# An attention, MoE and soft-MoE kernel on one core: v in fp16 parts everywhere, scores from fp16 parts of q and k, and a second expert layer on four column groups

## The chip, the core and the metric

The kernel runs on one core of one Trainium2 chip. The metric is the device time of one execution in microseconds (us); the time before is 681.06 us, the median of three runs (677.28 to 685.23). A core has TensorE (PE, matmuls, its weight loads shown as PEld), VectorE (DVE), ScalarE (ACT), GpSimd (POOL) and SyncE (SP, which only issues DMAs here). The clock of PE that the chip grants stands beside the busy times as a share of 2.4 GHz; the two levels are 1.2 and 2.4 GHz.

## What is computed

Three stages, one after the other, on 4 batches of 576 tokens (2304 in all) with 8 heads of 64:

```python
scores = scale * np.matmul(q, k.transpose(0, 1, 3, 2))
thresh = np.max(scores, axis=-1, keepdims=True) - tau
scores = np.where(scores >= thresh, scores, -1000000000.0)
attn = np.exp(scores - scores.max(-1));  attn /= attn.sum(-1) + 1e-9
x = np.matmul(attn, v)                       # -> [2304, 512]
h = x @ w_in                                 # [512, 2048]
x = np.maximum(0.01 * h, h) @ w_out          # [2048, 512]
logits = x @ phi                             # 8 experts x 4 slots
slot_input = softmax(logits, over tokens).T @ x
slot_out[e] = np.maximum(slot_input[e] @ w1[e], 0) @ w2[e]    # w1, w2: 8 x 512 x 1024
out = softmax(logits, over slots) @ slot_out
```

All inputs are fp32 (`w_in` and `w_out` arrive as 64 bit numbers and are made into fp32 on the chip). fp32 accuracy is kept either by fp32 matmuls or by splitting an operand into an fp16 part (hi) and the fp16 rest (lo) and multiplying hi by hi, hi by lo and lo by hi.

## The kernel before

The tokens are cut into 18 tiles of 128. Batches are 4.5 tiles long, so tiles 4 and 13 hold rows of two batches. For each tile `attention` computes 8 heads in 4 pairs, `feed` computes the hidden layer (48 matmuls of 512 columns, L1331, in 4 quarters of 12) and the logits, and `block` updates the running sums over two tiles. After the last tile a tail computes the expert layers for the 32 slots and the output.

Each operation is added with a priority, a cost and the engines that may run it; a planner (`Plan.schedule`) then fixes the order of the instructions on every engine, by the costs given and the table `O` of constants. On the chip each engine goes through its own list in that order and waits where an operand or a buffer isn't ready. The buffers are named by tags with a fixed number of slots.

What the change touches:

- **Scores.** `load_qk` loads q and k of one batch and one pair (640 KB, tag `qk`, 8 slots). `heads` multiplies them in fp32, two heads at a time on the upper and lower 64 rows of PE (L1100), into a PSUM tile S of 2 x 512. `ends` does the same for the last 64 keys (L1071). VectorE takes the maximum (L1109), ScalarE applies the threshold (L1125).
- **Weights times v.** `own(t)` says which pairs go by `by_pe`: all four for tiles 0 to 3 (`P0`, `TP=4`), pair 3 alone for the others (`P1`). `by_pe` transposes the weights on PE in fp32 (9 of 128 x 128, L1159), applies exp while ScalarE copies them back (L1164), and multiplies with v in fp32 (5 matmuls a head, L1176). The other pairs go by `by_dma`: exp in place (L1192), a cast to fp16 hi (L1202 on VectorE or L1203 on ScalarE), three subtractions on GpSimd for lo (L1213, 512, 128 and 512 elements long as the trace counts them), a DMA transpose of each head issued by SP (L1226, 9 blocks of 128), and 14 fp16 matmuls of 65 columns a head (L1250). The tag `ah` for hi and lo has 2 slots, `aT` for what is transposed has 3.
- **v.** `split_v` makes the fp16 parts (`vx`) and fp32 copies (`vr`, `vs`) as the pairs need them.
- **Tail.** `load` fetches 64 blocks of 512 KB of w1 and w2 into slots of the tags in `BIG` (27 of them: wh, qk, r, e2, ae, ah), as they become free; the first layer (L1685) multiplies k by k for four experts on four groups of 32 columns of PE; the second layer (L1753) has 32 operations of 4 matmuls, each operation for one expert, that is one group of columns. Blocks of w_out (`wot`) lie in slots of the tags in `SM`, until L1641 has used them.

Of the kernel before, what the change touches and what calls it, by code (L numbers as in the profile page):

```python
# [359 lines left out]
def emit(tc, a, out, dbg=None, opt=None):  # L360
# [73 lines left out]
    for n, p_, k in (  # L434
# [4 lines left out]
        ("qk", "main", O["QK"]), ("vr", "main", O["VR"]), ("vx", "main", O["VX"]), ("vs", "main", O["VS"]),  # L439
# [36 lines left out]
    def dump(name, b, sel, prio=1e9):  # L476
        if dbg and name in dbg:
# [36 lines left out]
    gate8, rt = const([P, 1]), const([P, 1])  # L514
    dve_op(
        P0, 80,
        lambda: dve.tensor_scalar(
            out=gate8.ap, in0=gate.ap, scalar1=0.125, scalar2=None, op0=ALU.mult
        ),
        r=[gate], w=[gate8],  # L520
    )
    dve_op(
        P0, 80,
        lambda: dve.tensor_scalar(
            out=rt.ap, in0=taup.ap, scalar1=8.0, scalar2=None, op0=ALU.mult
        ),
        r=[taup], w=[rt],
    )
# [6 lines left out]
    )  # L535

# [289 lines left out]
    for c in range(FF // P):  # L826
# [21 lines left out]
        pe_op(PQ, 440, f, r=[w, ident], w=[tp])  # L848
# [15 lines left out]
        pe_op(PQ, 850, f, r=[wt, phi], w=[wpp])  # L864
# [102 lines left out]
    qk = {}  # L967

    def load_qk(b, prio, step):
        for pr in range(4):  # L970
            raw = qk[b, pr] = pl.buf("qk", [P, 2, KX])
            dma(
                prio + pr * step, t_dma(P * 2 * KX * 4),
                (lambda pr, raw: lambda dq: dq.dma_start(out=raw.ap, in_=a["qk"][b, pr]))(pr, raw), w=[raw],
            )

    vtiles, vfs, vrs_of = {}, {}, {}

    own = lambda t: O["P0"] if t < O["TP"] else O["P1"]
# [25 lines left out]
    def split_v(b, pr, prio, vr):  # L1005
        sv = svs[b]
        vf = lambda: vr.ap[:, :, 0:D]
# [10 lines left out]
        if any(pr not in own(t) for t in tiles_of(b)):  # L1018
            vx = vtiles[b, pr] = pl.buf("vx", [P, 2, 10, D + 2], F16)
            va = lambda w: vx.ap[:, w, :, 0:D]  # L1020
            q = prio + (O["VD"] if any(pr in own(t) for t in tiles_of(b)) else 0.0)
# [13 lines left out]
            fm = lambda eng: lambda: eng.memset(vx.ap[64:, 1, 8:, 0:D], 0.0)  # L1035
            add_alt(q, [("pool", 180, fm(pool)), ("dve", 110, fm(dve))], w=[(vx, 1)])
            for w in range(2):
                pool_op(
                    q, 100, (lambda w: lambda: pool.memset(vx.ap[:, w, :, D : D + 1], 1.0 - w))(w),
                    w=[(vx, 2 + w)],  # L1040
                )
        if any(pr in own(t) for t in tiles_of(b)):
            vs = vfs[b, pr] = pl.buf("vs", [P, 2, D + 2])
            fc = lambda eng: lambda: eng.tensor_copy(out=vs.ap, in_=vr.ap[:, 8:])
            add_alt(prio, [("pool", 300, fc(pool)), ("dve", 150, fc(dve))], r=[vr], w=[vs])
            fm = lambda eng: lambda: eng.memset(vr.ap[:, 0:8, D : D + 1], 1.0)
            add_alt(prio, [("pool", 100, fm(pool)), ("dve", 110, fm(dve))], w=[(vr, 1)])
            fm = lambda eng: lambda: eng.memset(vs.ap[:, :, D : D + 1], 1.0)
            add_alt(prio, [("pool", 100, fm(pool)), ("dve", 110, fm(dve))], w=[vs])
            for i in range(2):  # L1050
                fm = lambda eng, i=i: lambda: eng.memset(
                    vs.ap[64 - 64 * i : 128 - 64 * i, i, 0 : D + 1], 0.0)
                add_alt(prio, [("pool", 100, fm(pool)), ("dve", 110, fm(dve))], w=[vs])
            vrs_of[b, pr] = vr
# [8 lines left out]

    def ends(t, prio):
        Tp = pl.buf(("misc",), [P, H, KT], F32, "Tp")
        Ts, tn = pl.buf("T", [P, H, KT]), pl.buf("tn", [P, H])

        def f():
            for r0, r1, b, o in regs_of(t):
                for pr in range(4):  # L1070
                    pe.matmul(  # L1071
                        out=Tp.ap[r0:r1, 2 * pr : 2 * pr + 2], lhsT=qk[b, pr].ap[:, 0, o : o + r1 - r0],
                        rhs=qk[b, pr].ap[:, 1, KW:KX], start=(pr == 0), stop=True, skip_group_check=True,
                    )

        pe_op(prio, 900 * len(tile_parts(t)), f, r=[qk[b, pr] for b in tile_parts(t) for pr in range(4)], w=[Tp, Ts, tn])
        act_op(prio, t_act(512), lambda: act.activation(out=Ts.ap, in_=Tp.ap, func=AF.Copy), r=[Tp], w=[Ts])
        dve_op(
            prio, 607,
            lambda: dve.tensor_reduce(out=tn.ap, in_=Tp.ap, axis=AX.X, op=ALU.max, negate=True),  # L1080
            r=[Tp], w=[tn],
        )
        dve_op(
            prio, 75,
            lambda: dve.tensor_scalar(
                out=tn.ap, in0=tn.ap, scalar1=rt.ap[:, 0:1], scalar2=None, op0=ALU.add
            ),
            r=[rt], w=[tn],
        )
        return Ts, tn  # L1090

    def heads(t, pr, prio, ae, flat, Ts, tn):
# [3 lines left out]
        def f():  # L1096
            for r0, r1, b, o in regs_of(t):
                for i in range(2):
                    h = slice(64 * i, 64 * i + 64)
                    pe.matmul(  # L1100
                        out=ps.ap[r0:r1, i], lhsT=qk[b, pr].ap[h, 0, o : o + r1 - r0],
                        rhs=qk[b, pr].ap[h, 1, 0:KW], start=True, stop=True, skip_group_check=True,
                    )

        pe_op(prio, 900 * len(tile_parts(t)), f, r=[qk[b, pr] for b in tile_parts(t)], w=[ps])
# [6 lines left out]
        for i in range(2):  # L1112
# [3 lines left out]
                    out=th.ap[:, i : i + 1], in0=nm.ap[:, i : i + 1], scalar1=rt.ap[:, 0:1],  # L1116
# [13 lines left out]
        tail = lambda: two(ae.ap[:, 2 * KW :]) if flat else ae.ap[:, :, KW:S]  # L1130
        pl.add(
# [15 lines left out]
    def by_pe(t, pr, p, parts, regs, Ts, tn, xa, xbuf):  # L1147
# [5 lines left out]
        def turn(c0, c1, key):  # L1153
# [3 lines left out]
            def f():  # L1157
# [11 lines left out]
        for i, (c0, c1) in enumerate(((0, 4), (4, 8), (8, 9))):  # L1169
            turn(c0, c1, i)  # L1170
# [698 lines left out]
```

## Time and profile before

| | us |
|---|---|
| median of 3 runs | 681.06 |
| the profiled execution | 686.13 |
| its span, first to last instruction | 684.3 |
| PE busy | 612.7 (90% of the span) |
| DVE busy | 406.3 (59%) |
| ACT busy | 399.6 (58%) |
| POOL busy | 172.8 (25%) |
| granted PE clock, mean | 0.939 |

A busy time is that in which at least one instruction of the engine runs. Instructions of one engine overlap, on PE by much: a matmul of 512 fp16 columns is shown with 385 ns, while the next one starts 217 ns after it. So what a group of matmuls takes from PE is read from the time at which the next group starts. SPq stands for SP's list of DMAs.

### The profile page before, as it was taken

Reading aid. Unit: us, or ns where it says so; the run is one execution under the profiler, and the core shown is the slowest. Engines: PE = TensorE matmul, PEld = TensorE weight load, DVE = VectorE, ACT = ScalarE, POOL = GpSimd, SP = SyncE. Lnnn points to the kernel's source line nnn. Section 1 sums busy time; section 2 is a strip of 40 time slices with the busy share of each in tenths; the row PEclk is TensorE's granted clock in tenths of the full one; section 3 lists DMA queues with packets and bytes.
Section 4 is the critical chain, followed back from the end, with each engine's and each line's share of the span. In section 5 each row is a group of like instructions: output and inputs, shape, how many; then the busy total and the mean of one; then the engine's idle time right before and its main releaser. Section 6 shows DMA issues by size and latency. Waiting matters only on the chain.

```text
span 684.3 us, 13565 instructions
## 1 busy us (share of the span) xinstructions
PE 612.7 (90%) x5212; PEld 369.2 (54%) x5212; DVE 406.3 (59%) x992; ACT 399.6 (58%) x745; POOL 172.8 (25%) x253
## 2 busy tenths in 40 slices
PE   4898887999879999999999898999999988489995
PEld 1666555776445656565555554655556643224552
DVE  3978869656757586599886555565767343310011
ACT  4887667776747677688786637576666522211022
POOL 0200100200323256245355323263363200200000
PEclk8798988999989999999999889999999999689997
DMA  8965410455998687899697659677669966839995
GB/s 321 375 221 181 129 61 17 139 159 164 163 214 152 115 143 127 186 190 200 121 177 119 114 89 201 132 133 131 105 123 213 203 131 177 267 109 413 409 408 215
DMA packets 203297, 123.94 MB, mean 181 GB/s; under 512 B 179168, under 2 KB 179680, under 8 KB 203232
## 3 DMA queue, kind: packets, MB, share of 16 engines
q1 hardware_dynamic: 199488, 114.02, 69.1%
q10 hardware_dynamic: 3744, 9.05, 5.5%
q8 instruction: 41, 0.67, 0.4%
q14 instruction: 24, 0.20, 0.1%
HBM read 70.48 MB, written 8.91 MB: 116 GB/s over the span
## 4 chain that ended last, share of the span: by engine, by line
PE 69%; ACT 11%; DVE 7%; DMA 6%; issue 3%; SPq 1%; POOL 1%; ACTq 0%; POOLq 0%; DVEq 0%
PE h L1331 23%; PE S L1100 9%; PE X L1176 6%; PE X L1753 6%; PE X L1250 5%; PE eT L1159 3%; PE misc L1176 3%; DMA aT<-ah 2%; ACT e L1164 2%; PE S L1685 2%; DMA rT<-r 2%; PE misc L1071 2%; PE misc L1525 2%; PE misc L862 2%; ACT g L1343 2%
## 5 line engine op out<-in xcount | busy, mean ns | idle before, releaser
L1331 PE MATMUL h<-wh,xT 128*128 128x512 f16 x864 | 215.0, 385 | 7.5 <-ACT g L1343 6.6
L1213 POOL TENSOR_TENSOR ah<-ae,ah 128x512 f16<-128x512 f32 (+1 forms) x126 | 120.6, 984 | 162.3 <-DVE ah L1202 130.7
L1331 PEld LDWEIGHTS <-xT 128*128 128x128 f16 x864 | 80.4, 100 | 101.7 <-issue 35.2
L1125 ACT ACTIVATE ae<-S,th 128x512 f32<-128x512 f32 x144 | 94.3, 686 | 17.5 <-POOL ah L1213 7.0
L1109 DVE TENSOR_REDUCE nm<-S 128x2 f32<-128x1024 f32 x72 | 87.7, 1219 | 28.2 <-PE S L1100 28.1
L1100 PE MATMUL S<-qk 64*128 64x512 f32 (+1 forms) x320 | 89.1, 690 | 9.6 <-DMA qk<-in_qk 5.9
L1343 ACT ACTIVATE g<-h,c 128x512 f32<-128x512 f32 x72 | 49.5, 687 | 70.0 <-PE h L1331 65.0
L1164 ACT ACTIVATE e<-eT,c,c 128x512 f32<-128x512 f32 (+1 forms) x90 | 60.1, 668 | 27.9 <-PE eT L1159 27.8
L1350 DVE CAST r<-g 128x512 f16<-128x512 f32 x57 | 27.8, 487 | 67.4 <-ACT g L1343 62.8
L1250 PEld LDWEIGHTS <-aT 128*128 128x128 f16 (+1 forms) x1344 | 49.7, 103 | 25.0 <-issue 14.6
L1250 PE MATMUL X<-vx,aT 128*128 128x65 f16 (+1 forms) x1344 | 54.4, 196 | 4.5 <-DMA aT<-ah 4.5
L1159 PE MATMUL eT<-c,ae 128*128 128x128 f32 x270 | 49.7, 296 | 8.7 <-ACT e L1164 8.1
L1192 ACT ACTIVATE ae<-ae,c,c 128x1152 f32<-128x1152 f32 x42 | 56.6, 1348 | 0.8
L1159 PEld LDWEIGHTS eT<-c,ae 128*128 128x128 f32 x270 | 34.1, 151 | 28.8 <-ACT e L1164 18.0
L1176 PE MATMUL X<-vr,e 128*128 128x65 f32 (+1 forms) x352 | 47.1, 281 | 0.0
L1357 DVE TENSOR_TENSOR r<-g,r 128x512 f16<-128x512 f32 x56 | 44.3, 791 | 3.9 <-ACT r L1352 3.0
L1134 POOL TENSOR_TENSOR ae<-T,th 128x128 f32<-128x128 f32 x33 | 15.4, 468 | 122.6 <-DVE th L1115 61.4
L1176 PEld LDWEIGHTS X<-vr,e 128*128 128x128 f32 (+1 forms) x352 | 45.0, 200 | 2.3 <-issue 1.2
L1202 DVE CAST ah<-ae 128x1152 f16<-128x1152 f32 x33 | 25.7, 779 | 20.2 <-ACT ae L1192 14.3
L1100 PEld LDWEIGHTS S<-qk 64*128 64x128 f32 (+1 forms) x320 | 23.2, 190 | 26.7 <-ACT ae L1125 7.8
L1115 DVE TENSOR_SCALAR th<-nm,c,tn 128x1 f32<-128x1 f32 x144 | 31.8, 264 | 0.8
L1376 PE MATMUL misc<-c,rT 128*128 128x64 f16 x288 | 19.1, 191 | 9.6 <-DMA rT<-r 9.2
(288 smaller groups left out, 911.0 us busy)
## 6 DMA issues: line engine op xcount, KB each, us to landing
wh<-in_w SPq DMA_DIRECT2D x21, 512.0 KB, 10.1
qk<-in_qk SPq DMA_DIRECT2D x15, 640.0 KB, 5.5
qk<-in_w SPq DMA_DIRECT2D x18, 512.0 KB, 8.0
r<-in_w_in SPq DMA_DIRECT2D x16, 512.0 KB, 4.1
r<-in_w SPq DMA_DIRECT2D x13, 512.0 KB, 10.2
rT<-in_w_out SPq DMA_DIRECT2D x25, 256.0 KB, 3.4
scr<-w SPq DMA_DIRECT2D x16, 256.0 KB, 3.3
vr<-in_v SPq DMA_DIRECT2D x9, 330.0 KB, 4.4
```

The costliest lines, as they stand in the source:

```text
L1100: pe.matmul(out=ps.ap[r0:r1, i], lhsT=qk[b, pr].ap[h, 0, o : o + r1 - r0], rhs=qk[b, pr].ap[h, 1, 0:KW], start=True, stop=True, skip_group ...
L1109: lambda: dve.tensor_reduce(out=nm.ap, in_=ps.ap, axis=AX.X, op=ALU.max, negate=True),
L1125: (lambda i: lambda: act.activation(out=main()[:, i], in_=ps.ap[:, i], func=AF.Prelu, bias=th.ap[:, i : i + 1], scale=1.0, alpha=2.0**90))(i),
L1159: pe.transpose(tp.ap[:, c - c0], ae.ap[:, c * P : (c + 1) * P], ident.ap)
L1164: lambda: act.activation(out=eT.ap[:, c0:c1], in_=tp.ap, func=AF.Exp, bias=nt.ap[:, 0:1], scale=gate8.ap[:, 0:1]),
L1176: pe.matmul(out=xa(2 * pr + i)[r0:r1], lhsT=eT.ap[:, c, r0:r1], rhs=(vfs[b, pr].ap[:, i] if c == 8 else vrs_of[b, pr].ap[:, c])[:, 0 : D + 1],
L1192: lambda: act.activation(out=ae.ap, in_=ae.ap, func=AF.Exp, bias=nt.ap[:, 0:1], scale=gate8.ap[:, 0:1]),
L1213: lambda: pool.tensor_tensor(out=ah.ap[:, h, w0 : w0 + c1 - c0], in0=ae.ap[:, h, c0:c1], in1=ah.ap[:, h, c0:c1], op=ALU.subtract),
L1250: pe.matmul(out=xa(2 * pr + i)[r0:r1], lhsT=w()[:, r0:r1], rhs=vtiles[b, pr].ap[:, wv, cv, 0 : D + 1], start=(n == 0 and 2 * pr + i in (0, ...
L1331: pe.matmul(out=hp.ap, lhsT=xT.ap[:, wx * 4 + k], rhs=wh(k, j, ww), start=(n == 0), stop=(n == 11),)
L1343: (lambda g, hp, j: lambda: act.activation(out=g.ap, in_=hp.ap, func=AF.Prelu, alpha=0.01, scale=hsc.ap[:, j : j + 1]))(g, hp, j),
L1357: fg = lambda eng, j, g: lambda: eng.tensor_tensor(out=r[j](1), in0=g.ap, in1=r[j](0), op=ALU.subtract)
```

## The change

1. `own`, `P0` and `P1` are gone. `K0='dhdh'` and `K1=('dddd',)` say for each pair how it goes: `d` is `by_dma`, `h` is `by_pe` with an fp16 hi and lo of the transposed weights and of v, `f` is the former fp32 way, which no pair uses. So in tiles 0 to 3 pairs 0 and 2 go by DMA and pairs 1 and 3 by `h`; from tile 4 on all four go by DMA.
2. From batch 1 on (`QB=1`) q and k are loaded into a new tag `qr` with one slot, and `split_qk` scales and splits them into fp16 hi and lo. Scores are then three fp16 products. The scale is that of the batch and pair (`rscale`, `rtau`).
3. w2 in the tail: one operation holds four experts, and the loop over them is the inner one. Nine blocks of w1 are fetched in halves into the tags of `SM`; `qr` is added to `BIG`.
4. The constants of the planner and some costs are others (`NW`, `XH`, `AT`, `AE`, `AH` and `QK` stay, `VX` 5, `VR` 4, `VS` 1, `VH` 4).

```diff
+        K0='dhdh', K1=('dddd',), VH=4, QB=1, QR=1, XH=1,
...
+            raw = pl.buf("qr" if fine(b) else "qk", [P, 2, KX])
...
+    def split_qk(b, pr, p, raw):
+        am = tmp([P, 2])
+        dve_op(
+            p, t_dve(2 * KX), lambda: dve.tensor_reduce(
+                out=am.ap, in_=raw.ap, axis=AX.X, op=ALU.max, apply_absolute_value=True),
...
+        pw2 = pow2_two(p, am)
...
+        for n in range(2):
+            act_op(
+                p, t_act(KX) + 90, (lambda n: lambda: act.activation(
+                    out=q.ap[:, 0, n], in_=raw.ap[:, n], func=AF.Copy, scale=sc.ap[:, n : n + 1]))(n),
...
+            dve_op(
+                p, P2(t_dve(KX)), (lambda n: lambda: dve.scalar_tensor_tensor(
+                    out=q.ap[:, 1, n], in0=raw.ap[:, n], scalar=sc.ap[:, n : n + 1], in1=q.ap[:, 0, n],
+                    op0=ALU.mult, op1=ALU.subtract))(n),
...
+    PROD = ((0, 0), (0, 1), (1, 0))
...
+                todo = PROD if fine(b) else (None,)
+                for n, w in enumerate(todo):
...
+                    for i in range(2):
+                        h = slice(64 * i, 64 * i + 64)
+                        pe.matmul(
+                            out=ps.ap[r0:r1, i], lhsT=q[h, 0, o : o + r1 - r0], rhs=k[h, 1, 0:KW],
...
+            if kind(t, pr) != "d":
                 by_pe(t, pr, p, parts, regs, Ts, tn, xa, xbuf)
             else:
                 by_dma(t, pr, p, parts, Ts, tn, weigh)
...
+        w = [load(a["w1"][e, k][:, n], T0 - 7.5, [P, 512], "c2", SM, 512) for n in range(2)]
...
-                for j in range(4):
-                    q = hts[G]
-
-                    def f(j=j, n=n, G=G, q=q, w=ws[j], hf=hf):
-                        for c in range(4):
+                def f(n=n, G=G, ws=ws, hf=hf):
+                    for c in range(4):
+                        for j in range(4):
```

`pow2_two` (new) finds the power of two under each of the two maxima: a matmul with the identity, five small VectorE instructions in a row, of which each needs the one before, and a second matmul with ones between the fourth and the fifth.

In numbers of instructions in the built programs: DMA transposes of weights 84 before and 128 now, fp16 matmuls of 65 columns with v 1344 and 2256, fp32 ones 320 matmuls and none, PE transposes of weights 270 and 72. VectorE has 994 instructions before and 1183 now, ScalarE (its DMAs with it) 730 and 771, GpSimd 255 and 321.

**Place 1, VectorE, tile 8 or so.** In the changed program a split of q and k lies between the maxima (`nm<-S`, L1218 there, L1109 before) of a pair of heads:

```order
L1019 TENSOR_REDUCE tmp<-qr 128x2
L1218 TENSOR_REDUCE nm<-S_76 128x2
L541 TENSOR_REDUCE tmp<-misc 2x1
L1465 TENSOR_TENSOR xT<-eT,xT 128x512
L544 TENSOR_SCALAR tmp<-tmp 2x1
L1511 CAST r<-g 128x512
L549 TENSOR_SCALAR tmp<-tmp 2x1
L1363 CAST ah<-ae 128x2x576
L554 TENSOR_SCALAR tmp<-c_83,tmp 2x2
L1518 TENSOR_TENSOR r<-g,r 128x512
L1218 TENSOR_REDUCE nm<-S_77 128x2
L563 COPY tmp<-misc 128x2
```

The small steps of `pow2_two` (L541 to L563) are spread between the work of the tiles; L541 and L563 each need a matmul first. Before, none of these rows but L1218, L1465, L1511, L1363 and L1518 was there.

**Place 2, PE, second expert layer.** Before, a row is one expert's operation, and its four matmuls write the same group of 32 rows of X:

```order
L1753 MATMUL X_8015<-wh_8013,ae_7201 32x256 x4
L1753 MATMUL X_8015<-wh_8020,ae_7201 32x256 x4
L1753 MATMUL X_8015<-wh_8039,ae_7201 32x256 x4
L1753 MATMUL X_8015<-r_8058,ah_7217 32x256 x4
L1753 MATMUL X_8015<-wh_8064,ah_7217 32x256 x4
```

Now four blocks of four experts take turns, and each next matmul writes another group:

```order
L1921 MATMUL X_9311<-r_9115,ae_8451 32x256
L1921 MATMUL X_9311<-r_9119,ae_8451 32x256
L1921 MATMUL X_9311<-r_9124,ae_8451 32x256
L1921 MATMUL X_9311<-qk_9215,ae_8451 32x256
L1921 MATMUL X_9311<-r_9115,ae_8451 32x256
```

**Place 3, SP, from the last DMA transpose on.** Before, the blocks of w1 and w2 follow as slots of `BIG` come free:

```order
L1673 DMA r<-in_w 128x1024 x2
L1366 DMA_TRANSPOSE rT<-r 128x8x128
L1673 DMA wh<-in_w 128x1024 x4
L1673 DMA r<-in_w 128x1024 x4
L1673 DMA qk<-in_w 128x1024 x8
L1673 DMA wh<-in_w 128x1024
```

Now halves (128x512) into slots of `SM` stand between them:

```order
L1834 DMA r<-in_w 128x1024
L1834 DMA wh<-in_w 128x1024 x4
L1834 DMA rT<-in_w 128x512 x4
L1834 DMA r<-in_w 128x1024 x4
L1834 DMA w<-in_w 128x512 x3
L1834 DMA raw<-in_w 128x512
L1834 DMA vr<-in_w 128x512
L1834 DMA w_9170<-in_w 128x512
L1834 DMA U<-in_w 128x512 x2
L1834 DMA vr<-in_w 128x512 x3
```

18 halves in all, of which the four into rT and one before them do not need a block of w_out to be used up first.

## Rows read from the trace of the kernel before

**Rows 1.** Windows by stage: us, busy us (instructions) by engine, PE clock, DMA share, GB/s.
```profile
11.00:117.00 106.00, 84.47 (x485) 60.15 (x484) 85.77 (x220) 80.99 (x160) 10.74 (x36) 0.84 0.52 178
117.00:243.00 126.00, 115.95 (x1035) 76.58 (x1034) 83.45 (x210) 84.89 (x165) 29.74 (x40) 0.97 0.73 155
243.00:531.00 288.00, 279.69 (x2732) 166.01 (x2728) 197.77 (x458) 199.27 (x352) 121.86 (x150) 0.98 0.82 148
531.00:581.00 50.00, 45.00 (x411) 24.71 (x411) 20.70 (x51) 16.78 (x34) 4.50 (x5) 1.00 0.78 169
581.00:611.00 30.00, 17.35 (x124) 7.99 (x122) 7.51 (x21) 6.59 (x15) 5.08 (x15) 0.66 0.65 203
611.00:626.00 15.00, 14.83 (x136) 5.21 (x137) 0.95 (x9) 1.09 (x2) 0.00 (x0) 1.00 0.81 314
626.00:672.00 46.00, 45.47 (x281) 23.78 (x276) 3.57 (x13) 5.00 (x10) 0.00 (x0) 1.00 0.99 395
672.00:684.30 12.30, 4.86 (x13) 2.41 (x12) 3.10 (x5) 3.70 (x8) 0.00 (x0) 0.65 0.50 192
```
**Rows 2.** Windows of line L1331 alone, 48 matmuls a tile: PE and PEld.
```profile
0.00:243.00 243.00, 49.63 (x192) 18.20 (x192) 0.92 0.64 171
243.00:531.00 288.00, 131.05 (x528) 48.55 (x528) 0.98 0.82 148
```
**Rows 3.** Timeline of PE inside tile 9: start us, us shown, line, out<-in, instructions.
```profile
297.37 0.38 PE L567 MATMUL misc<-tmp,c 1*128 1x1 f32 x2
297.68 0.66 PE L1159 MATMUL eT<-c,ae 128*128 128x128 f32 x4
298.17 1.06 PE L1071 MATMUL misc<-qk 128*128 128x128 f32 x8
299.06 0.60 PE L1250 MATMUL X<-vx,aT 128*128 128x65 f16 x14
299.51 0.81 PE L1331 MATMUL h<-wh,xT 128*128 128x512 f16 x3
300.25 1.13 PE L1100 MATMUL S<-qk 64*128 64x512 f32 x4
301.31 2.12 PE L1331 MATMUL h<-wh,xT 128*128 128x512 f16 x9
303.26 0.60 PE L1159 MATMUL eT<-c,ae 128*128 128x128 f32 x4
...
306.49 1.00 PE L1176 MATMUL misc<-vr,e 128*128 128x65 f32 x8
...
307.64 1.13 PE L1100 MATMUL S<-qk 64*128 64x512 f32 x4
```
**Rows 4.** Groups of DVE by shape, 240 to 530 us: busy us, mean ns of one | idle before.
```profile
L1109 DVE TENSOR_REDUCE nm<-S 128x2 f32<-128x1024 f32 x45 | 54.8, 1218 | 12.9 <-PE S L1100 12.8
L1030 DVE TENSOR_TENSOR vx<-vr,vx 128x640 f16<-128x640 f32 x5 | 4.3, 860 | 0.0
...
L575 DVE RECIPROCAL tmp<-c 128x1 f32<-128x1 f32 x4 | 0.6, 156 | 0.0
```
**Rows 5.** One line, 243 to 531 us: duration ns min/median/max.
```profile
L1357 DVE TENSOR_TENSOR r<-g,r x33: 670/692/1615, 242.6 to 528.6; 128x512 f16<-128x512 f32 x33
```
**Rows 6.** Groups of POOL by shape, 240 to 530 us.
```profile
L1213 POOL TENSOR_TENSOR ah<-ae,ah 128x512 f16<-128x512 f32 x69 | 82.6, 1200 | 93.7 <-DVE ah L1202 71.1 <-issue 10.9 <-ACT ah L1203 7.8
L1213 POOL TENSOR_TENSOR ah<-ae,ah 128x128 f16<-128x128 f32 x35 | 20.6, 588 | 0.0
```
**Rows 7.** DMA transposes of line L1226, 240 to 530 us: issue ns min/median/max.
```profile
L1226 SPq DMA_TRANSPOSE aT<-ah x68: 1242/1312/3433, 240.4 to 527.6; - x68
```
**Rows 8.** Timeline of SP in the tail, loads of w1 and w2.
```profile
595.39 2.08 SPq L1673 DMA_DIRECT2D r<-in_w  x4
613.11 3.93 SPq L1673 DMA_DIRECT2D qk<-in_w  x8
```
**Rows 9.** Windows of line L1753 alone, second expert layer.
```profile
626.00:672.00 46.00, 41.21 (x256) 20.98 (x256) 1.00 0.99 395
```

More of the change, by code (lines that the diff above doesn't have):

```diff
@@ L1070, in f @@
                 for pr in range(4):
[L1071 to L1077, printed above, removed]
+                    todo = PROD if fine(b) else (None,)
+                    for n, w in enumerate(todo):
+                        q, k = (qk[b, pr].ap, qk[b, pr].ap) if w is None else (qk[b, pr].ap[:, w[0]], qk[b, pr].ap[:, w[1]])
+                        pe.matmul(
+                            out=Tp.ap[r0:r1, 2 * pr : 2 * pr + 2], lhsT=q[:, 0, o : o + r1 - r0],
+                            rhs=k[:, 1, KW:KX], start=(pr == 0 and n == 0), stop=(n == len(todo) - 1),
+                            skip_group_check=True,
+                        )
+        pe_op(
+            prio, 760 if fine(tile_parts(t)[0]) else 1000, f,
+            r=[qk[b, pr] for b in tile_parts(t) for pr in range(4)], w=[Tp, tn] + ([] if still else [Ts]),
+        )
+        rt = by_rows(prio, t, "rt", lambda b: rtau[b])
+        if not still:
+            act_op(prio, t_act(512), lambda: act.activation(out=Ts.ap, in_=Tp.ap, func=AF.Copy), r=[Tp], w=[Ts])
         dve_op(
@@ L1083, in ends @@
         dve_op(
[L1084 to L1088, printed above, removed]
+            prio, 75, lambda: dve.tensor_tensor(out=tn.ap, in0=tn.ap, in1=rt.ap, op=ALU.add), r=[rt], w=[tn]
         )
@@ L1170, in by_pe, with f @@
             turn(c0, c1, i)
+        if kind(t, pr) == "f":
+            for i in range(2):
+                def f(i=i):
+                    for r0, r1, b in regs:
+                        for n, c in enumerate((*range(4 * i, 4 * i + 4), 8)):
+                            pe.matmul(
+                                out=xa(2 * pr + i)[r0:r1], lhsT=eT.ap[:, c, r0:r1],
+                                rhs=(vfs[b, pr].ap[:, i] if c == 8 else vrs_of[b, pr].ap[:, c])[:, 0 : D + 1],
+                                start=(n == 0 and 2 * pr + i in (0, H - 1)), stop=(n == 4), skip_group_check=True,
+                            )
+                pe_op(
+                    p + 0.22, 5 * 252, f, r=[(eT, (k, x[0])) for k in (i, 2) for x in regs] + [v[b, pr] for b in parts for v in (vfs, vrs_of)],
+                    w=[xbuf(2 * pr + i)],
+                )
+            return
@@ L1679, in emit @@
         for k in range(4):
-            ws = [load(a["w1"][4 * G + j, k], T0 - 7, [P, 2, 512]) for j in range(4)]
+            ws = [w1_of(4 * G + j, k, G and 4 * k + j >= 16 - O["HF"]) for j in range(4)]
             def f(k=k, ws=ws, h1=h1):
```

307 lines of the change are left out of this document (214 added, 93 removed).

## The prediction

> **What bounds the kernel now.** I read first the windows by stage [rows 1, 2]: line L1331 has 48 matmuls a tile, so its counts tell where tiles end. The feeds of tiles 0 to 3 (192) are done at 243 us, those of tiles 4 to 14 (528) at 531, the last 144 at 581. After that come the last tile's logits, block and w_out product (to 611, PE clock 0.66), the first expert layer (to 626), the second (to 672) and the last output. In the body, 243 to 531, PE is busy 279.69 of 288 us, 97%, at clock 0.98, while DVE and ACT stand at 69% each and POOL at 42% [rows 1]: PE is the bound there, and a microsecond taken from PE is a microsecond gained until another engine comes near. The front is different: from 11 to 117 us DVE is busy 85.77 of 106 us (81%) and PE 80% at clock 0.84; only from 117 to 243 does PE lead with 92% [rows 1]. From 626 to 672 PE is busy 45.47 of 46 us and the DMAs move 395 GB/s [rows 1], so there two things end together. Inside a tile I read PE's timeline and take for each group the time to the next start [rows 3].
>
> **PE in the body, per tile.** *Pair 3.* Before: nine fp32 transposes at (298.17-297.68)/4 = 0.12, 1.1 us, and two heads, each 307.64-306.49 = 1.15 for eight of its ten matmuls, at least 2.3; 3.4 together [rows 3]. After: two heads of 14 fp16 matmuls at (299.51-299.06)/14 = 0.032, 0.9 to 1.0 us [rows 3]. Saved 2.4, and I take 2.3. *Scores.* An operation of four fp32 matmuls takes 301.31-300.25 = 1.06; four of them a tile, one per pair [rows 3]. After it is three products, each for two heads on the two halves of the rows. An fp16 matmul of 512 columns takes (303.26-301.31)/9 = 0.217 [rows 3]. If the two halves run side by side, as the fp32 ones must (four passes of one head alone would be 4 x 0.217 = 0.87, two heads 1.73, and 1.06 is shown), it is 3 x 0.217 = 0.65; if not, 1.30. I take 0.75, near the lower end, since the pairs of fp32 matmuls come so near to one head's time, with some loss as these have. Saved 4 x 0.31 = 1.24; bounds 1.6 saved to 1.0 lost. *The last 64 keys.* Eight fp32 ones 299.06-298.17 = 0.89; after, twelve small fp16 ones, 0.05 each from the two prices above, 0.65: 0.24 saved. *pow2_two.* Two tiny fp32 matmuls for each split; such a one takes 297.68-297.37 = 0.31 [rows 3]; 24 in all, some 0.5 a tile lost. Net 2.3 + 1.24 + 0.24 - 0.5 = 3.3 us a tile, over 11 tiles 36: PE falls from 279.7 to about 243 us in the body.
>
> The price of the added small matmuls is where a rule speaks against the change. The Trainium skill, "TensorE: Matmul & The Clock Gate", section "Back-to-back issue gap", gives about 81 ns for each matmul of 128 columns in a sustained stream of weight loads and matmuls. The trace shows 32 ns for those of 65 columns with a new weight block each [rows 3]; by the page's figure the 28 of a tile would cost 11 x 28 x 0.049 = 15 us more over the body, an estimate that would put the time near 663. The trace's own duration decides, and the sum goes by it.
>
> **VectorE.** Each of the 12 splits of q and k adds a maximum over 1280 elements, 1.218 x 1.25 = 1.5 us by L1109; two subtractions of 640, as L1030, 0.86 each; and eleven small steps at 0.156 or somewhat more, about 2 [rows 4]. That is 5.2 us, 62 in all. By their place in VectorE's list five lie up to tile 4 and seven after it. With the other changes (copies and casts of v for the front's pairs, fewer steps for `vs`) the counts on VectorE's list by the durations of such rows give +34 us up to the last feed of tile 3 (169 to about 203 between 11 and 243 us) and +33 in the body (198 to 231). None of it is free: in the body DVE comes within 12 us of PE. ScalarE gets the hi parts, some +10 us in the body (199 to 209), below DVE. GpSimd has the lo parts of one more pair a tile, 2 x 1.2 + 0.59 = 3.0 us [rows 6], +33: 122 to 155 us. SP issues 88 transposes in the body instead of 66, 1.31 us each [rows 7]: 115 us, and the DMA share of 0.82 [rows 1] rises; it stays off the path as long as a transposed pair is there before its matmuls, which the planner puts behind other work of PE.
>
> The wait that the change adds is that of the split: the two steps of `pow2_two` that need a matmul stand in VectorE's list between maxima and the halves of r (place 1). Where such a matmul comes late, the maxima behind it wait, with them ScalarE's threshold and the next S. PE's own list has 0.3 us steps, so a late one costs some tenths each time, 14 times in the body. I put that into the share below.
>
> **The sum by stage.** *Front (11 to 243).* PE loses about 39 us of fp32 work of the pairs 0 and 2, but DVE has 34 more, and it was the bound of the first half. 203 us at 85% is 239, so the last feed of tile 3 ends at 11 + 239 = 250. Bounds: 92%, as PE has it between 117 and 243, 232; 81%, as DVE has it in the first half, 262. *Body.* PE needs 243, DVE 231. With one engine at 69% the other reached 97%; with both at 80% (the first half) neither came above 81 [rows 1]. Between these I take 91% for PE, 267 us instead of 288; DVE then stands at 86%. Bounds: 250 (PE at 97%) and 288 (DVE at 80%). *Tiles 15 to 17.* 50 us, unchanged: 34 to 45 us of it are feeds and the splits are over. *Tail.* It lasts 684.3-581 = 103.3. The chain to 611 is the same work, 30. Before, SP issued four loads at 595.39 and the next eight only at 613.11 [rows 8], a gap while it waited for slots; 0.524 MB at 395 GB/s is 1.33 us a block, and 395 x 46 + 314 x 13 = 22.3 MB [rows 1] are some 40 of the 64 blocks that came from then on. After (place 3) `qr` holds a block, about five halves go out ahead, and 13 more where blocks of w_out are used up, which PE does within the chain to 611. So about 8 blocks move from behind 613 to before it: 10 to 12 us earlier. That is worth nothing if PE can't follow: L1753 is busy 41.21 of the 46 us [rows 9] for 128 matmuls of 32 rows. Now four groups of columns take turns (place 2); as the four groups of one step can run beside each other, a quarter of it to a half, 10 to 20 us, and PE trails the loads no more, which gives another 8 us at its end. I take 103.3 - 11 - 8 = 84.5; bounds 82 and 95 (only the latter half of one of the two). Sum: 250 + 267 + 50 + 84.5 = 651.5 us of span, against 684.3. The profiled execution is 686.13, 1.8 more than its span, and the median of the runs, 681.06, is 0.9926 of it; (651.5 + 1.8) x 0.9926 = **648 us**.
>
> **Rivals.** *A, the forecast,* 648, own range 630 to 667; chance 0.54. *B, nothing else binds:* the front gains its full 11 us (232), the body takes 250, the tail 82: 614 of span, by the same factor 611. For it: 97% was reached once; against: DVE would stand at 92%, which it does in no stage. Chance 0.14. *C, the body gains nothing:* VectorE can't do more than 80%, or the halves of scores don't run side by side; body 288, 672.5 of span, 669 us. For it is the first half of the front. Chance 0.18, 0.07 of it within 1% of before. *D, the other side:* GpSimd's added subtractions hold up VectorE. The same subtraction of r on VectorE, x33, took 670 ns at least and 1615 at most [rows 5], and the difference is near one subtraction on GpSimd, 1200 ns [rows 6]. GpSimd is busy 42% of the body and would be near 58%. In the body VectorE has some 132 instructions with two operands, 12 a tile; if each waits half a subtraction on average, 79 us, DVE has 310 and even at 98% the body takes 317: 701.5 of span, 698 us. It decides from a body of 306 on (688 us), that is from 60 to 70 us of such waits. Against it: the median of those 33 is 692, so most of them met nothing. Chance 0.08. The Trainium skill, "SBUF — State Buffer", section "Who interferes with whom", states an exclusive lock on the ports that VectorE and GpSimd share; by that rule waits of a whole instruction must be seen, and the trace agrees (1615 against 670). *E, the tail stays:* the halves find their slots no earlier, since w_out's blocks are freed by the same late chain; 95 instead of 84.5, 659 us; chance 0.06.
>
> **Range and chances.** The likeliest is A. The range 612 to 676 reaches over B's and C's ends and leaves out D and about 0.1 beside it. A measurement of this kernel can tell about 1% from no change, here 674 to 688. Faster by over 1%: A, B, E and most of C, 0.83. Within 1%: 0.08. Slower: D and a little, 0.09.
>
> **What would show it.** Right: the last feed of tile 3 near 250, of tile 14 near 517, of tile 17 near 567; PE about 91% and DVE about 86% busy in that body; an S operation from start to start near 0.75 us; no stretch of 18 us without loads on SP; the second layer's line busy 10 to 20 us and no longer 41. Wrong: an S operation of 1.3 us (C); subtractions of r whose median, not only the maximum, is over 1 us (D); loads that start again only with the first layer (E); a DVE over 92% (B). What would make all of it wrong is a late split: ScalarE or PE standing for S of a new batch while the maxima wait behind `pow2_two`.

## The result and the profile after

The changed kernel takes 644.42 us (median of 4 runs, 642.01 to 646.18) against 681.93 us for the kernel before in the same comparison: a ratio of 0.945, 95% interval 0.939 to 0.952. The forecast was 648 in a range of 612 to 676. A second set of runs of the same program on another chip gave 643.1 us, ratio 0.953 (0.950 to 0.957). Here and below a ratio and its interval are taken from the executions in a chip's faster state alone, while medians are over all executions, so the two need not agree. The total came out; of its stages the front was 17 us off and the last two 4 us each, and the reason given for the body turned out to be only half of it.

The stages after, by windows cut where the 192nd, 720th and 864th matmul of the hidden layer (line L1492 now) start; the columns are as in [rows 1], busy us of PE, PEld, DVE, ACT and POOL, then PE clock, DMA share and GB/s:

```profile
11.00:117.00 106.00, 78.14 (x582) 52.54 (x582) 96.73 (x245) 97.73 (x197) 38.48 (x57) 0.71 0.80 241
117.00:233.00 116.00, 102.97 (x1051) 59.53 (x1052) 105.17 (x262) 85.89 (x152) 47.34 (x54) 0.91 0.72 154
233.00:499.00 266.00, 237.87 (x2810) 131.93 (x2808) 234.62 (x551) 207.49 (x344) 143.10 (x170) 1.00 1.01 182
499.00:553.00 54.00, 47.72 (x511) 25.84 (x509) 26.72 (x65) 22.55 (x46) 15.41 (x15) 1.00 1.04 209
553.00:584.00 31.00, 19.43 (x141) 8.74 (x143) 7.57 (x21) 6.61 (x15) 5.10 (x15) 0.72 0.90 299
584.00:597.00 13.00, 13.00 (x120) 4.14 (x116) 0.84 (x8) 1.19 (x2) 0.00 (x0) 1.00 1.04 416
597.00:629.00 32.00, 25.14 (x288) 12.11 (x276) 3.93 (x13) 4.79 (x10) 0.00 (x0) 0.96 1.02 414
629.00:642.00 13.00, 3.86 (x13) 1.97 (x12) 2.83 (x5) 3.75 (x8) 0.00 (x0) 0.76 0.51 201
```

Each line answers to one of [rows 1]. In the body PE's share fell from 97 to 89% and DVE's rose from 69 to 88%: no engine is full any more. The stages beside the forecast, with the second profile of the same program ("again"):

| us | before | forecast | after | again |
|---|---|---|---|---|
| to the last feed of tile 3 | 242.2 | 250 | 233.1 | 236.0 |
| body, tiles 4 to 14 | 288.3 | 267 | 266.0 | 265.3 |
| tiles 15 to 17 | 50.3 | 50 | 54.2 | 54.2 |
| tail | 103.5 | 84.5 | 88.7 | 86.7 |
| span | 684.3 | 651.5 | 642.0 | 642.1 |

What a group of the new matmuls takes is read as in [rows 3], from the timeline of PE inside one tile (start us, us shown, line, out<-in, instructions, and in brackets the idle time before it):

```profile
283.46 0.82 PE L1206 MATMUL S<-qk 64*128 64x512 f16 x6
284.21 1.47 PE L1492 MATMUL h<-wh,xT 128*128 128x512 f16 x6
...
286.72 0.38 PE L536 MATMUL misc<-c,tmp 128*2 128x128 f32 x2 [0.60 <-DVE tmp L1019]
287.03 1.47 PE L1492 MATMUL h<-wh,xT 128*128 128x512 f16 x6
...
290.69 0.61 PE L1411 MATMUL X<-vx,aT 128*128 128x65 f16 x14
291.14 0.81 PE L1492 MATMUL h<-wh,xT 128*128 128x512 f16 x3
```

A score operation takes 284.21-283.46 = 0.75 us, the tiny matmul of `pow2_two` 287.03-286.72 = 0.31, and 14 matmuls with v 291.14-290.69 = 0.45, that is 0.032 each: all three as forecast. Where PE still waits in the body, it is mostly for the one PSUM slot of the hidden layer that ScalarE's copy (L1504) empties (columns: engine and line, what it waited for, us in total, times, longest):

```profile
PE h L1492 <- ACT g L1504: 15.4, 24, 1.4
```

Near the end of the body the chain of waits runs over three engines in turn (start us, us, what):

```profile
444.93 0.60 DVE tn L1187
445.53 1.13 DVE nm L1218
446.66 0.49 DVE tn L1191
447.18 0.28 DVE th L1224
447.50 0.04 issue
447.55 1.27 ACT ae L1234 x2
448.82 0.04 issue
448.87 0.82 PE S L1206 x6
449.69 0.77 PE h L1492 x3
450.48 0.70 ACT g L1504
```

A maximum on VectorE lets ScalarE apply the threshold, which frees the PSUM tile for PE's next scores, behind which stand the next hidden-layer matmuls, whose copy on ScalarE PE needs again. Summed over the pieces of this view from 432.85 to 499 us (it goes back no further than 432.85), PE has 32 of 66 us, DVE 18, ACT 12. Before, between 243 and 531, PE had 183 of the 236 us of the 195 longest pieces.

### The profile page after: what moved, and what is told of

It is laid out like the page before. It is cut to its first block, busy times and chain, and to the rows that moved or that the text cites. A ratio compares the mean times of both kernels' runs of the same rounds, so it can differ in the third digit from the quotient of the medians.

```text
span 642.0 us, 14640 instructions
## 1 busy us (share of the span) xinstructions
PE 533.0 (83%) x5514; PEld 299.0 (47%) x5514; DVE 482.5 (75%) x1181; ACT 431.3 (67%) x774; POOL 250.4 (39%) x319
## 5 line engine op out<-in xcount | busy, mean ns | idle before, releaser
L1374 POOL TENSOR_TENSOR ah<-ae,ah 128x512 f16<-128x512 f32 (+1 forms) x192 | 183.0, 980 | 162.4 <-DVE ah L1363 79.0
L1492 PE MATMUL h<-wh,xT 128*128 128x512 f16 x864 | 214.1, 382 | 22.9 <-ACT g L1504 21.6
L1492 PEld LDWEIGHTS <-xT 128*128 128x128 f16 x864 | 77.9, 98 | 107.6 <-issue 39.4
L1234 ACT ACTIVATE ae<-S,th 128x512 f32<-128x512 f32 x144 | 93.5, 684 | 18.7 <-DVE th L1224 10.0
L1218 DVE TENSOR_REDUCE nm<-S 128x2 f32<-128x1024 f32 x72 | 87.5, 1215 | 13.2 <-PE S L1206 12.8
L1411 PEld LDWEIGHTS <-aT 128*128 128x128 f16 (+1 forms) x2016 | 74.4, 101 | 36.3 <-issue 21.1
L1206 PE MATMUL S<-qk 64*128 64x512 f16 (+3 forms) x440 | 77.0, 483 | 16.3 <-ACT ae L1234 10.2
L1353 ACT ACTIVATE ae<-ae,c,c 128x1152 f32<-128x1152 f32 x64 | 86.3, 1348 | 1.2
L1504 ACT ACTIVATE g<-h,c 128x512 f32<-128x512 f32 x72 | 49.2, 683 | 46.3 <-PE h L1492 45.0
L1411 PE MATMUL X<-vx,aT 128*128 128x65 f16 (+1 forms) x1792 | 73.9, 195 | 5.7 <-DVE x L1447 3.6
L1518 DVE TENSOR_TENSOR r<-g,r 128x512 f16<-128x512 f32 x61 | 48.2, 792 | 2.3 <-ACT r L1513 1.7
L1363 DVE CAST ah<-ae 128x1152 f16<-128x1152 f32 x50 | 39.5, 790 | 7.2 <-DMA aT<-ah 4.2
L1511 DVE CAST r<-g 128x512 f16<-128x512 f32 x39 | 18.2, 466 | 20.8 <-ACT g L1504 19.6
L1518 POOL TENSOR_TENSOR r<-g,r 128x512 f16<-128x512 f32 x11 | 14.3, 1304 | 42.2 <-DVE r L1511 21.3
L1322 POOL TENSOR_TENSOR ah<-e,ah 128x512 f16<-128x512 f32 (+1 forms) x17 | 16.1, 958 | 31.1 <-ACT ah L1317 26.3
L891 PE MATMUL misc<-c,w 128*128 128x32 f32 x128 | 22.2, 325 | 3.7 <-ACT w L881 2.1
L1047 ACT ACTIVATE qk<-qr,tmp 128x640 f16<-128x640 f32 x24 | 19.0, 819 | 9.2 <-DVE tmp L1027 9.2
L891 PEld LDWEIGHTS misc<-c,w 128*128 128x128 f32 x128 | 20.7, 245 | 9.2 <-ACT w L881 3.3
L875 PE MATMUL h<-c,w 128*128 128x128 f32 x64 | 15.0, 372 | 11.3 <-DVE c L829 5.6
```

Of the source, the lines that this page charges most:

```text
L891: pe.matmul(out=wpp.ap, lhsT=wt.ap[:, k], rhs=phi.ap[:, k], start=(k == 0), stop=(k == 3))
L1206: pe.matmul(out=ps.ap[r0:r1, i], lhsT=q[h, 0, o : o + r1 - r0], rhs=k[h, 1, 0:KW], start=(n == 0), stop=(n == len(todo) - 1), skip_group_c ...
L1218: lambda: dve.tensor_reduce(out=nm.ap, in_=ps.ap, axis=AX.X, op=ALU.max, negate=True),
L1234: (lambda i: lambda: act.activation(out=main()[:, i], in_=ps.ap[:, i], func=AF.Prelu, bias=th.ap[:, i : i + 1], scale=1.0, alpha=2.0**90))(i),
L1353: lambda: act.activation(out=ae.ap, in_=ae.ap, func=AF.Exp, bias=nt.ap[:, 0:1], scale=rs.ap[:, 2 * pr : 2 * pr + 1]),
L1363: ("dve", P2(t_dve2(2 * S)), lambda: dve.tensor_copy(out=ah.ap[:, :, :S], in_=ae.ap)),
```

## The experiments

Twelve kernels were run, each also profiled. Eleven are the changed kernel with one edit, or two in the tail; one is the changed kernel as it is. Stage times are those of the profiled executions, cut as above. The runs were made on three chips: the four with added work on one (kernel before there: 678.6 us), `u_w2`, `u_half`, `u_s32` and `u_p3` on a second (681.1), the others on a third (675.6). The control shows how far stages differ between two profiles of one program: 3 us in the front, 1 in the body, 2 in the tail.

### The control

> The changed kernel once more, unaltered, on the chip of the three runs beside it: stages (to the feed of tile 3, body, tiles 15 to 17, tail) 233, 266, 54, 89 us as in its first profile, each within 2 us. If the front or the body differ by 6 us and more, then the +6 us in the front of the runs with added TensorE and GpSimd work, where hardly any was added, are the spread between executions and not an effect.

Ratio 0.953; 236.0, 265.3, 54.2 and 86.7 us: the front and the tail 3 and 2 us off, the body 0.7, so the front missed the 2 us expected and stayed below the 6. Against the control the fronts of `s_pe` and `s_pool` (239.6 and 239.5) are 3.5 us longer, which is little more than that spread. The control was on the third chip only; front and body of `u_w2` and `u_half` (233.7 and 266.5, 233.1 and 265.7), where only the tail is edited, extend it to the second. The first chip has no such control.

### Work added on one engine, and work taken from VectorE

The order of instructions stays; a step is repeated with the same result, or one is shortened.

```diff
 s_pe:   todo = PROD if fine(b)       ->  ((0, 0), (0, 0)) + PROD if fine(b)     # scores
 s_dve:  tensor_reduce(nm, ps)        ->  tensor_reduce(nm, ps[:, :, 0:256]); tensor_reduce(nm, ps)
 s_act:  Prelu(ae[0]); Prelu(ae[1])   ->  Prelu(ae[0]) twice; Prelu(ae[1])
 s_pool: 128-element subtraction L1374 ->  the same, twice
 r_dve:  tensor_reduce(nm, ps)        ->  tensor_reduce(nm, ps[:, :, 0:256])
```

> Every score operation of the fp16 kind gets two more products that are overwritten (the first product is made three times), 0.25 us each by the 0.75 us that three take in the trace after: +0.5 us in 44 operations between the feeds of tiles 3 and 14, +22 us of TensorE there, +6 in the tiles behind; the order is the same. Theory (TensorE is still what the body waits for, at 89% busy, with VectorE close behind): the body grows from 266 by 16 to 22 us, the total by 20 to 28. Rival 1 (VectorE is the bound of the body now): 0 to 6 us. Rival 2 (the DMAs, share 1.01, are the bound): about 0.

> Every maximum over the scores is preceded by one over half of its columns, whose result is overwritten: about 0.63 us by half of 1.218, 28 of them up to the feed of tile 3 (+18 us of VectorE) and 44 in the body (+28); the order is the same. Theory (TensorE first, VectorE close behind): body +10 to 18, front +14 to 18. Rival 1 (VectorE is the bound): body +25 to 28, front +18. Rival 2 (the DMAs): body about 0. The maximum stands between a score and its threshold, so some of it may show as a wait of ScalarE.

> The threshold of the first head of every pair is applied twice, with the same result: 0.68 us each, 28 up to the feed of tile 3 (+19 us of ScalarE) and 44 in the body (+30); the order is the same. ScalarE was busy 207 of 266 us. Theory: body +3 to 10, as the hidden layer's copies (the wait that TensorE's gaps show most) come later. Rival (ScalarE in order is what holds the hidden layer's PSUM, and so TensorE): body +20 to 30.

> GpSimd makes the 128-element subtraction of each pair that goes by DMA twice, with the same result: 0.59 us each, 44 in the body (+26 us of GpSimd, 143 to 169 of 266); the order is the same. Theory: 0 to 4 us, through later DMA transposes. Rival (case D of the prediction, GpSimd's port holds up VectorE): each added subtraction delays a VectorE step by part of its time, VectorE's busy time grows by 8 us or more, and the body by as much.

> The maxima over the scores read half of the columns only (the maximum over the other half is left out): -0.63 us of VectorE for each, 28 to the feed of tile 3 (-18 us), 44 in the body (-28). Theory now (VectorE leads front and body, TensorE is next at 89%): front -10 to -18, body -8 to -20, since TensorE's 238 us at 97% need 245. Rival (what the longer maxima cost was only the delay of one step in a chain, and TensorE leads): body -5 us at most.

Ratios to the kernel before: `s_pe` 0.976 (0.965 to 0.987), `s_dve` 1.018 (1.006 to 1.029), `s_act` 0.999 (0.994 to 1.004), `s_pool` 0.977 (0.966 to 0.987), `r_dve` 0.946 (0.942 to 0.950). The windows of the bodies, in the order control, `s_pe`, `s_dve`, `s_act`, `s_pool`, `r_dve`, columns as above:

```profile
236.00:501.30 265.30, 237.59 (x2810) 132.00 (x2809) 233.92 (x551) 207.08 (x344) 142.53 (x170) 1.00 1.01 182
```
```profile
239.60:513.80 274.20, 255.87 (x2998) 140.98 (x2997) 236.01 (x551) 207.65 (x344) 141.15 (x168) 1.00 0.96 176
```
```profile
251.20:542.30 291.10, 242.67 (x2809) 133.47 (x2808) 257.54 (x594) 208.22 (x344) 142.00 (x169) 0.99 0.94 164
```
```profile
247.00:527.90 280.90, 239.42 (x2809) 134.82 (x2808) 235.98 (x550) 234.64 (x387) 140.85 (x168) 1.00 0.94 171
```
```profile
239.50:515.80 276.30, 240.15 (x2809) 133.53 (x2808) 235.32 (x550) 207.71 (x344) 165.39 (x214) 0.99 0.97 175
```
```profile
231.50:496.80 265.30, 236.70 (x2810) 131.69 (x2809) 213.65 (x550) 206.62 (x344) 142.67 (x169) 1.00 1.02 182
```

Against the control, each edited engine's busy time and the body changed by

| | busy of the engine | body | share |
|---|---|---|---|
| `s_pe` | +18.3 | +8.9 | 0.5 |
| `s_dve` | +23.6 | +25.8 | 1.1 |
| `s_act` | +27.6 | +15.6 | 0.6 |
| `s_pool` | +22.9 | +11.0 | 0.5 |
| `r_dve` | -20.3 | 0.0 | 0 |

The number of `s_dve` may be too high for a typical execution: the profiled one took 688.5 us, the other three 680.9 to 681.9. If all of these 7 us lie in the body, the share is 0.8.

If one engine were the bound, work added on the others would cost little. Here every addition costs, GpSimd's too, which is busy 54%. `s_dve` by itself would have made VectorE the bound (rival 1 of its expectation, +25 to 28), and that was my theory when I wrote the expectation of `r_dve`. As the whole account it fell: 20 us less on VectorE, 81% busy instead of 88, left the body where it was, and the front only 4.5 us shorter than the control's instead of 10 to 18. So VectorE is not alone in holding the body: something else takes 265 us as well. `s_pe` (8.9) stands between its theory (16 to 22) and the rivals, `s_act` (15.6) between its theory (3 to 10) and its rival (20 to 30), and `s_pool` (11.0) is above the 0 to 4 of its theory.

What the other limit is, the runs do not show. With the shorter maximum the chain of waits over the last 66 us has 6 us of DVE and 38 of PE, where after the change it had 18 and 32: another path of the same length stood behind. PE's wait for the PSUM slot of the hidden layer did not shrink either (control, then `r_dve`, each in its body):

```profile
PE h L1492 <- ACT g L1504: 16.0, 24, 1.6
PE h L1492 <- ACT g L1504: 16.5, 22, 1.4
```

Two accounts fit: one chain through four lists in fixed order, in which a delay anywhere is handed on in part; or several limits at about the same place, VectorE at 88% being one. A longer maximum takes time of VectorE and delays a step of the chain at once, so `s_dve` and `r_dve` do not separate them. That the planner's order is what holds the body is argued and not shown. A second slot for the hidden layer, or another step of the chain made shorter, was not tried.

`s_pool` also settles rival D of the prediction: 23 us more of GpSimd left VectorE's busy time at 235.3 us against 233.9. What GpSimd costs, the 11 us, goes for the larger part through ScalarE: its threshold (L1234) writes into the slot of `ae` that GpSimd's subtraction (L1374) still reads, and waits for it (control, then `s_pool`, each in its body):

```profile
ACT ae L1234 <- POOL ah L1374: 6.7, 11, 1.3
ACT ae L1234 <- POOL ah L1374: 21.7, 23, 2.2
```

PE's wait for that threshold (S L1206) grows with it, from 0.8 to 5.1 us. The other way, through the DMA transposes that need the subtractions, is the smaller one: PE, VectorE and ScalarE together wait 4.0 us for a transposed pair, against 1.5 in the control.

### The tail

```diff
 u_w2:    for c in range(4): for j in range(4): matmul   ->  for j in range(4): for c in range(4): matmul
 u_half:  HF=9                                           ->  HF=0
 u_tail:  both
```

> The second expert layer alone back: the four matmuls of one expert follow each other in the same group of columns (the two inner loops swapped); all else and the order of the loads is as in the changed kernel. Theory of the prediction (TensorE trailed the loads): the layer's line goes from 20 us busy to about 41, and the time grows by 6 to 10 us. Rival (the loads alone end the layer): below 2 us.

> No halves of w1 (HF=0): the nine blocks are fetched whole into the slots of BIG, later; everything else by the same table. Theory of the prediction (about eight blocks move ahead): the loads stand idle again while slots are held, and the time grows by 8 to 12 us, all of it behind the last feed. Rival (the slot of qr and the two half sets hide it): below 3 us.

> Both tail edits undone: no halves (HF=0) and the second layer expert by expert. Alone they cost 3 and 5 us of the tail in their profiles, 14.8 us separate the tails of the two kernels. Theory (loads later and TensorE's trailing add up): tail 96 to 98 us against 88.7, so 6 us of the 14.8 come from elsewhere: the slot of qr and the chain in front of it. Rival (they cover for each other, and together are the whole gain): tail 101 to 104.

Ratios 0.972 (0.958 to 0.986), 0.974 (0.959 to 0.990) and 0.965 (0.960 to 0.969). The tails took 91.8, 94.0 and 97.7 us; the control, on the chip of `u_tail`, 86.7. The second layer alone, in windows that begin with its first matmul, in the order control, `u_w2`, `u_half`, `u_tail`:

```profile
599.50:629.60 30.10, 23.49 (x280) 11.50 (x272) 3.92 (x13) 4.79 (x10) 0.00 (x0) 1.00 1.03 416
```
```profile
594.00:633.00 39.00, 37.09 (x280) 20.73 (x275) 3.93 (x13) 4.79 (x10) 0.00 (x0) 1.00 0.89 361
```
```profile
593.70:634.00 40.30, 30.06 (x273) 13.16 (x272) 3.76 (x13) 3.81 (x8) 0.00 (x0) 0.92 1.03 414
```
```profile
599.40:639.40 40.00, 38.45 (x273) 21.32 (x272) 3.76 (x13) 3.81 (x8) 0.00 (x0) 1.00 1.03 414
```

These lines say more than the tails of single profiles. With PE's loops back (`u_w2`) the layer takes 39.0 us with PE at 95% and the DMAs at 361 GB/s: PE is the bound. Without the halves (`u_half`) it takes 40.3 us at 414 GB/s with PE waiting: the loads are the bound. With both undone it is 40.0. So each edit alone is worth about nothing in this layer, and both together 10 us, because they lift two limits that lie at the same place. The layer of `u_half` moves 4.2 MB more than the control's (40.3 us at 414 GB/s against 30.1 at 416), which is 8 blocks of 0.524 MB, as many as the prediction had moving ahead. The tails of the profiles hide the overlap: their single losses, 8 to 12 us in sum by the profile compared with, are near the 11.0 that `u_tail` lost, which is what the theory of adding up expected (96 to 98 for its tail). But in `u_w2` and `u_half` the chain ahead of the first expert layer ran 24.6 and 24.3 us, in the control 28.5, in `u_tail` 26.8. Why it differs is open. The medians agree with the layer: 651.4 and 654.7 us for one edit undone and 652.6 for both, against 643.1 for the control, so each alone costs about as much as the two together. (The profiled executions of `u_w2` and `u_half`, 647.7 and 648.4, are the shortest of four; the chips differ too.)

That `u_tail` still ends 5.8 us ahead of the kernel before (97.7 against 103.5) comes from neither edit. Both runs with the loops back keep one operation for four experts, and there line L1921 is not back at the 41 us expected (`u_w2`, `u_tail`):

```profile
594.00:633.00 39.00, 32.63 (x256) 17.99 (x255) 1.00 0.89 361
599.40:639.40 40.00, 34.67 (x256) 19.09 (x256) 1.00 1.03 414
```

So the grouping of experts may have a part in the 5.8 us; it was not undone in any run.

### Scores, pair 3 and the front

```diff
 u_s32:    QB=1                        ->  QB=4
 u_p3:     K0='dhdh', K1=('dddd',)     ->  K0='dhdf', K1=('dddf',), VS=2, VR=5, VX=4, VH=1
 u_front:  K0='dhdh'                   ->  K0='dfdf', VS=2, VH=1
```

Here the planner orders everything anew with constants that were set for the changed kernel, so these runs show the worth of a part only together with what another order costs.

> Scores in fp32 for all batches (QB=4), no splitting of q and k: TensorE +0.31 us in 56 score operations and +0.2 a tile, minus 24 small matmuls of the splits, some +14 us in all, +11 in the body; VectorE -62 us. Theory (TensorE leads the body, VectorE leads the front): front 3 to 10 us shorter, body 0 to 11 longer, total -5 to +8. Rival 1 (VectorE is the bound everywhere): total 20 to 40 us less. Rival 2 (the fp16 scores are the main gain): total +15 or more.

661.19 us as the median of 649.55, 659.90, 662.48 and 664.92, of which no interval is given. The profiled execution is one of the long ones, 662.48, with a span of 660.6 us:

```profile
244.00:523.70 279.70, 256.52 (x2762) 139.51 (x2760) 223.33 (x499) 196.84 (x334) 140.84 (x161) 0.99 0.98 173
```

PE has 19 us more in the body than in the control, VectorE 11 less, and this body is 14 us longer, with PE at 92%. But the execution is 13 us longer than the shortest of its own kernel, so neither the 14 us nor the 8 by which its front is longer can be put down to the edit. The shortest run is 5 to 6 us over the changed kernel (643.1 and 644.4), inside the -5 to +8 of the theory; it is a single one. Rival 1 (VectorE bounds everything, 20 to 40 us less) is out by every run. Rival 2 (+15 or more) is not decided: the long runs would fit it, the shortest does not. What the fp16 scores are worth stays open.

> Pair 3 by the former fp32 way again in all tiles, 0 to 17 (pairs 0 to 2 as in the changed kernel; one slot less for the parts of v, one more each for v and its fp32 copy). TensorE +2.4 us a tile against the fp16 matmuls, some +26 us in the body; DMA transposes a quarter fewer, GpSimd -33 us. Theory (TensorE leads the body): body +18 to 26, total +22 to 35. Rival (VectorE, GpSimd or the DMAs are the bound in the changed kernel): body 0 to 8.

696.49 us, ratio 1.038 (1.025 to 1.050): slower than the kernel before.

```profile
249.70:557.00 307.30, 273.50 (x2855) 162.12 (x2853) 230.50 (x559) 217.84 (x372) 114.21 (x142) 0.97 0.72 143
```

The body grew by 42 us where 18 to 26 were expected: PE has 36 us more, and is not full either (89%). The rival, 0 to 8 us, falls: the fp32 way of pair 3 costs PE more than the relief of GpSimd and the DMAs (share 0.72 instead of 1.01) brings. The fewer slots (`VX` 4 instead of 5, `VH` 1 instead of 4, the latter not named in the expectation) and another order are in this number too, so how much of the 42 us the DMA way of pair 3 is worth by itself is not shown.

> Pairs 1 and 3 of tiles 0 to 3 by the fp32 way instead of fp16 hi and lo from PE transposes (K0 dfdf; slots for the fp32 copies one more, for the fp16 ends three fewer). TensorE +1.4 us a pair after its transposes, at full clock 11 us up to the feed of tile 3 and more at 1.2 GHz; VectorE, ScalarE and GpSimd lose the casts and subtractions of eight pairs, some 6 to 8 us of VectorE. Theory (VectorE leads the front at 91%): front -5 to +3 us. Rival (TensorE at its lower clock leads it): +8 to +15.

658.69 us, ratio 0.976 (0.971 to 0.981), 16 us over the control. The front took 229.5 us, 6.5 less than the control's and 3.6 less than the first profile's: the theory's side. Eight pairs of fp32 work on PE showed no cost there. The loss came behind: the body +7.8, tiles 15 to 17 +11.8, of which one wait of PE for a transposed pair has 9.2 us:

```profile
PE X L1411 <- DMA aT<-ah: 9.2, 1, 9.2
```

The fp16 way of pairs 1 and 3 does not pay in the stage that it was priced in.

## Why the prediction was right, step by step

- **PE's work in the body: right.** 243 us forecast, 237.9 measured; 243 was at the clock of 0.98 before, at the 1.00 granted now it would be 238. The 0.75 us of a score operation, in bounds of 0.65 and 1.30, was the term most in doubt, and was met. The Trainium skill, "TensorE: Matmul & The Clock Gate", section "Back-to-back issue gap", gives about 81 ns for a matmul of 128 columns in a sustained stream; at that price the 14 matmuls of 65 columns with v would take 1.13 us, an estimate. The trace shows 0.45, as it did before.
- **VectorE, ScalarE and GpSimd: right or near.** 231 forecast against 234.6, 209 against 207.5, 155 against 143.
- **267 us for the body: right in size, in part by luck, the reason only in part.** PE had 5 us less work than forecast, and its share was 89% instead of 91; with one of the two alone the body would have been 261 or 272. The step took 91% between 97 and 80% because VectorE would come near, so it was argued as two nearly full engines. `r_dve` shows that VectorE's fullness is not all that keeps PE at 89%: with 81% the body was the same. And ScalarE, which I had set aside as "below DVE", and GpSimd, which I had only as rival D, cost half of what is added to them. The step should have read the chain of waits.
- **The front: the step that failed.** "203 us at 85%" had VectorE's work right (201.9 us busy between 11 and 233) and its share wrong: 91%, close to the bound of 92% that gave 232. The 17 us missed there (14 against the second profile) are the largest error of the sum. Why VectorE came to 91% and not 85 is open. `s_dve` (+15 us in the front for 18 added, in a long execution) and `u_front` (9 us less of VectorE, 4 to 6.5 us gained) fit a front that VectorE's steps lead; `r_dve` (-4.5 for 18 taken away, with 3 us between two profiles of one program) says that another limit stands close behind.
- **Tiles 15 to 17: 4 us too low.** "Unchanged" left out that more of their attention now falls behind the last feed of tile 14: PE has 511 instructions in that window where [rows 1] show 411, while in the body its count grew by 3% only.
- **The tail: right in sign, 2 to 4 us too high a gain.** No stretch of 18 us without loads is left, as there was from 595 to 613 [rows 8]; the longest in these rows is now the 7.6 us before 576, and after it halves follow each other:

```profile
566.37 2.08 SPq L1834 DMA_DIRECT2D r<-in_w  x4
576.07 1.28 SPq L1834 DMA_DIRECT2D w<-in_w  x3
...
581.89 0.97 SPq L1834 DMA_DIRECT2D vx<-in_w  x2
584.46 0.80 SPq L1834 DMA_DIRECT2D qk<-in_w  x2
```

  The second layer's line is busy 20 us instead of 41 [rows 9]:

```profile
597.00:629.00 32.00, 19.99 (x256) 9.37 (x256) 0.96 1.02 414
```

  I had added 11 us for the loads and 8 for PE, 19 in all. The runs show two limits of 39 and 40 us, of which both must go: the prediction said this of the loads (worth nothing "if PE can't follow") and still gave each a price of its own. `u_tail` puts the two at 11.0 us together, and 5.8 of the gain come from neither, so that the tail came out near 84.5 is in part luck. The bound of 95 for only a part of one of them lies near what the single edits left (91.8 and 94.0 us), but in those two runs the chain ahead was 4 us shorter; the layer itself had lost the whole gain.
- **The total: closer than its parts.** The errors of the stages are 17 and 1 us too high and 4 and 4 too low, 9.5 us of span together. The factor 0.9926, by which the profiled execution before lay above its median, took another 5 us off the forecast; the profiled execution after, 644.09 us, is no longer than its median. That 648 came within 4 us of 644.42 is in part luck.
- **The rivals.** B's front came true, its body did not. C (80%) didn't happen. D fell in the trace and on the chip. The subtraction of r on VectorE in the body, min, median and max in ns, beside [rows 5]:

```profile
L1518 DVE TENSOR_TENSOR r<-g,r x38: 669/692/1579, 235.1 to 497.3; 128x512 f16<-128x512 f32 x38
```

  The median didn't move with GpSimd at 54% instead of 42. The single long ones are still there, up to 1579 ns. The Trainium skill, "SBUF — State Buffer", section "Who interferes with whom", states an exclusive lock on the ports that VectorE and GpSimd share; the trace agrees in its longest subtraction, 1579 ns against 669 at least, and the median shows that most meet nothing. E fell with the SP rows above.

No version ran faster than the changed kernel with all of the work done: `r_dve`, at 637.5 us, leaves half of the maximum out.

## What to carry to other kernels

When a change brings a second engine within a few per cent of the bound, price the stage by the chain of waits, not by the fuller engine: here each microsecond added on any of four engines cost about half a microsecond or more, and 20 taken from VectorE gave nothing. Adding work alone would have named VectorE as the bound; taking some away showed that it is not the only one. When a stage has two limits at about the same place (here PE at 39 us and the loads at 40), undo the edits singly and together, and read the stage's own windows: alone each looks worthless, and the sums of single profiles, with another stage's spread in them, hide it. And a share of an engine taken between two observed ones is a guess of its own: 85 or 91% for VectorE were 17 us of this forecast.

## What the runs showed of the hardware that I had not expected

The DMA share rose to 1.01 in the body, the value that the tail shows while loads alone bind it (1.02 to 1.04). Yet the transposes landed as fast as before, in a median of 3.6 us, so the share alone doesn't tell that the queues hold the work up:

```profile
L1387 SPq DMA_TRANSPOSE aT<-ah x88: 1241/1300/3846, 234.2 to 500.0; - x88
DMA to landing us min/median/max: 3.2/3.6/8.8
```

Whether the DMAs set a floor under the body (it is 265.3 us in the control and in `r_dve`, at 1.01 and 1.02) was not tried. The waits speak against it: in the control's body PE waits once for a transposed pair, 1.5 us, its weight loads wait 2.2 us in all, and no wait of VectorE, ScalarE or GpSimd for a DMA is shown. And the granted clock of PE fell from 0.84 to 0.71 between 11 and 117 us, with PE busy 78 us of 106 instead of 84, in a front that still ended sooner.
